# Logit columns from whole weight words, by single-precision transposes with the turned block stationary

## The chip, the cores and the metric

One NeuronCore of a Trainium2 chip runs the whole kernel. The metric is the time of one execution on the device, in microseconds. The engines are TensorE (PE, matmuls, and PEld for its weight loads), VectorE (DVE), ScalarE (ACT), GpSimd (POOL) and SyncE (SP, which issues most DMAs).

## The reference

Three layers follow each other. Tokens are 4 sequences of 768, the model width is 384 (8 heads of 48).

```
# 1: linear attention with a complex decay, per head
S = a_n[t] * S + k[t] v[t]^T          # a_n: (a_re, a_im), clipped to magnitude 0.999
y[t] = q[t] . Re(S)
# 2: gated dense layer
x = y / rms(y) * rms_g
h = silu(x @ w_gate) * (x @ w_val)    # 384 -> 1536
x2 = h @ w_out                        # 1536 -> 384
# 3: one of 8 experts per token
logits = x2 @ moe2_w_gate             # 384 -> 8
e = argmax(logits);  p = softmax(logits)[e]
out = p * (relu(x2 @ w1[e]) @ w2[e])  # 384 -> 1024 -> 384
```

The weights of layer 2 arrive as 64-bit words that the kernel turns into single precision itself.

## The kernel before, in words

Tokens go through layers 1 and 2 in 12 units of 256. `elem(u)` computes decays and phases of unit u (ACT and DVE), spreads them over heads by DMAs (tile `QK`), `attention(u)` computes scores, outputs and normalised activations `xh`, `xl` (a rounded part and the rest, so that fast matmuls keep precision), `dense(u)` runs 12 features f of 128 hidden columns: stage 1 (L850) makes gate and value columns, stage 2 (L873) adds the product with the output weights into two PSUM accumulators. `finish(u)` stores the result and its expert's place. Then the eight experts run (L1299, L1317).

`convert` makes one block of 384x384 weights: DMA of the words into `st`; a memset of a `raw` buffer (L418); `top`, a widening copy of the high part (L395 on ACT, L397 on POOL); `join`, a shift and an or on DVE (L401), after which `raw` holds the whole single-precision word; `high`, the rounded copy into `w` (L406, L408); then the rest, either `low` on DVE or POOL (L411) or, for the blocks w00 and wo0, on PE (L430, L431) with ACT copies (L434). There are twelve blocks: w00 to w03 (gate), w10 to w13 (value), wo0 to wo3 (output). Only two `raw` buffers exist (NRAW=2), and other temporary tiles live in them too. The words of a block are fetched only when the block five places back has had its `top` (AHEAD=5).

From unit 1 on, stage 2 also makes the 8 expert logits: the output weights have 8 more columns, `w_out @ moe2_w_gate`. `logit_columns` makes them per output block: it turns the 9 sub-blocks (L450, each half of the split weight against the identity), copies them out (L454), multiplies with the gate matrix stationary (L460), copies (L465), turns the result back (L466), and writes its rounded part (L471) and the rest (L473). Unit 0 computes its logits from its output instead (L893, L897).

`keep_warm` (L1388) is 15 batches of 8 matmuls whose results nobody reads. Each needs a converted third of w00, w10, w01, w11 or w02; each has the last due time of all; all write one of the two PSUM buffers that the dense accumulators take later.

The order of all this is made by a planner, `Plan.issue`, in Python at build time. A step names engines with estimated costs, what it reads and writes, and a due time. At each turn the planner takes the engine on which some step could start earliest, and of the steps that could start there at that time the one with the lowest due time. A step gets its buffers when it is issued, if enough are free. A step's DMA goes into SP's queue in the planned order. Due times come from the constants in TUNE: for example a gate block's is T0 + 3 FT g + CG + C0g, and the logit columns' before was that of unit 1 plus LC + C3g. There are three PSUM banks of the kind `t` (`bank()`), two accumulators `a`, three buffers `m`.

Of the kernel before, what the change touches and what calls it, by code (L numbers as in the profile page):

```python
# [30 lines left out]
TUNE = dict(T0=771.62, PER=649.53, FT=4.77, A0=-422.97, A1=-431.72, A2=-35.5, E0=-1137.13, E1=236.14, E2=1375.6,  # L31
            E3=785.18, CG=483.05, CO=263.88, LC=-203.35, NRAW=2, AHEAD=5, DH=547.2, FI=-16.42, RP=-1165.15, TOL=0,
            S2L=28.66, NS=3, NH=3, HOP=0.2, W1=107.43, ATP=2, PA0=0, PA1=0.08, PE0=0, PE1=0.24, RG=1, LB=-24.77,
            EB=-56.74, RB=6.57, HB=-60.28, MB=-8.8, TB=10.11, AX=1, EE=-12.66, EL=7.32, BEG=0.7, DL=2, FN=8,
            FF=15, LW=1, LO=1, C00=-926.96, C01=-266.61, C02=382.08, C03=-259.36, C10=-529.22, C11=-373.75, C12=-583.49,
            C13=1773.0, C20=-587.24, C21=781.76, C22=1957.05, C23=2500.91, C30=583.92, C31=-599.84, C32=-15.96, C33=-423.27,
            AU1=282.87, AU2=-63.05, AU3=-787.85, AU4=-777.43, EU0=224.54, EU1=294.16, EU2=16.71, EU3=-24.77,
            EU4=41.45, EU5=43.43, AC=73.5, AC0=4.7)
# [212 lines left out]
def kernel(ctx, tc, qT, kT, reT, imT, v, wg, wv, wo, rg, w2g, w1, w2, out):  # L251
# [129 lines left out]
    def convert(name, src, n, due, by_pe):  # L381
# [59 lines left out]
    def logit_columns(w, due, after):  # L441

        pr, rows, pl, wts = bank(P, P), Buf(k_raw, shape=[P, P]), bank(P, P), Buf(k_raw, shape=[P, KD, KD, P])
        for q in range(KD):
            pw = bank(P, KD, P)

            def turn(e, q=q, pw=pw):
                for j in range(KD):
                    for i in range(2):
                        TE.matmul(pw.t[:, j, :], lhsT=w.t[:, q, i, j * P:(j + 1) * P], rhs=identr,  # L450
                                  start=(i == 0), stop=(i == 1))

            add((TE, 0.68), turn, r=[(w, 0), IDENTR] + lows(w), w=[pw], due=due, after=after)
# [3 lines left out]
        def prod(e):  # L457
            for j in range(KD):
                for q in range(KD):
                    TE.matmul(pr.t[LG * q:LG * (q + 1), :], lhsT=w2gt[:, j, :], rhs=wts.t[:, q, j, :],  # L460
                              start=(j == 0), stop=(j == KD - 1))

        n = LG * KD
        s = add((TE, 1.1), prod, r=[(wts, q) for q in range(KD)] + [W2G], w=[pr], due=due)
        add((A, act(P)), lambda e: e.activation(rows.t[:n], pr.t[:n], AF.Copy), r=[pr], w=[rows], due=due)  # L465
        add((TE, mm(P, 2)), lambda e: TE.transpose(pl.t[:, :n], rows.t[:n], ident[:n, :n]), r=[rows], w=[pl], due=due)  # L466

        def cols():
            return pl.t[:, :n].rearrange("p (q l) -> p q l", l=LG)[:, :, :E]

        add((A, act(3 * E)), lambda e: e.activation(w.t[:, :, 0, DM:], cols(), AF.Copy),  # L471
            r=[pl], w=[(w, 2)], due=due)
        add((V, dve(3 * E)), lambda e: e.tensor_tensor(  # L473
            out=w.t[:, :, 1, DM:], in0=cols(), in1=w.t[:, :, 0, DM:], op=ALU.subtract),
            r=[pl, (w, 2)], w=[(w, 3)], due=due)
        return [s]
# [853 lines left out]
    with tc.manual_schedule():  # L1330
# [39 lines left out]

        q = {0: elem(0)}
# [5 lines left out]
        for g in range(FF // WB):  # L1377
            for n, w in enumerate((wg, wv)):
# [3 lines left out]
                              g < TUNE["LO"]))  # L1382
# [174 lines left out]
```

## Time and profile before

| | us |
|---|---|
| median of 3 runs (lowest, highest) | 935.14 (935.04, 936.3) |
| profiled execution, whole | 936.97 |
| its span in the trace | 935.3 |
| PE busy | 896.5 |
| DVE, ACT, POOL busy | 613.2, 518.0, 181.6 |

All times inside the trace count from the span's start. A busy PE is not PE at its peak: matmuls overlap, and a group's own duration is longer than the distance to the next group's start. The cost of a group is therefore read as the distance from its start to the start of what follows it without a hole.

### The profile page before, as it was taken

The numbers are of one execution on the slowest core, as the hardware profiler recorded it, in microseconds if no ns is written. First come the engines' busy times: TensorE is split into PE (matmuls) and PEld (weight loads), VectorE is DVE, ScalarE is ACT, GpSimd is POOL, SyncE is SP. The second block draws the span as 40 slices with busy tenths as digits, with TensorE's granted clock in tenths as the row PEclk, the third lists the DMA queues.
The fourth block names the chain that finished last, engine by engine and source line by source line (L and its number), as shares of the span: only waits on it lengthen the run. The fifth ranks groups of instructions, "written<-read, shape, count | busy, mean of one in ns | idle before, by whom it ended". The sixth has DMA issues, their size and how long they took to land.

```text
span 935.3 us, 17743 instructions
## 1 busy us (share of the span) xinstructions
PE 896.5 (96%) x6747; PEld 863.5 (92%) x6747; DVE 613.2 (66%) x1528; ACT 518.0 (55%) x996; POOL 181.6 (19%) x226
## 2 busy tenths in 40 slices
PE   2699999999999999999999999999999999999996
PEld 2689999999999999999999999999989989999996
DVE  5699867778777768686868777546566642545510
ACT  7787876675655656655656565424426433544421
POOL 3232302010111010110201020101242532222121
PEclk9899999999999999999999999999999999999999
DMA  9955233423333140605050421102346753545200
GB/s 331 292 196 140 65 78 82 102 83 77 95 61 94 45 127 18 154 18 154 17 137 19 92 80 40 48 1 66 93 122 200 219 144 111 151 129 182 91 23 23
DMA packets 68363, 98.12 MB, mean 105 GB/s; under 512 B 16038, under 2 KB 49257, under 8 KB 68276
## 3 DMA queue, kind: packets, MB, share of 16 engines
q1 hardware_dynamic: 57316, 86.61, 32.9%
q0 software_dynamic: 10688, 9.95, 3.9%
q8 instruction: 54, 0.88, 0.4%
q10 hardware_dynamic: 272, 0.40, 0.1%
q14 instruction: 33, 0.27, 0.1%
HBM read 68.19 MB, written 10.15 MB: 84 GB/s over the span
## 4 chain that ended last, share of the span: by engine, by line
PE 68%; DVE 11%; issue 8%; DMA 5%; ACT 5%; POOL 2%; SPq 0%; POOLq 0%; DVEq 0%; ACTq 0%
PE m L850 25%; PE a L873 15%; PE a L1317 7%; PE m L1299 7%; PE t L680 4%; PE t L720 3%; DVE ee L541 2%; PE t L724 1%; DMA out_dram<-eo,idx 1%; PE t L698 1%; POOL out_dram L1325 1%; DMA QK<-qk 1%; DMA rawb<-in_w_dram 1%; DVE re L576 1%; DVE rs L785 1%
## 5 line engine op out<-in xcount | busy, mean ns | idle before, releaser
L850 PE MATMUL m<-xh,w 128*128 128x256 f32 x1728 | 276.6, 285 | 1.1 <-DVE s L862 0.6
L850 PEld LDWEIGHTS m<-xh,w 128*128 128x128 f32 x1728 | 234.6, 188 | 5.7 <-issue 3.4
L873 PE MATMUL a<-wo,hh 128*128 128x392 f32 (+1 forms) x576 | 151.8, 345 | 0.0
L850 PE MATMUL m<-xl,w 128*128 128x256 f32 x864 | 149.1, 281 | 0.0
L850 PEld LDWEIGHTS m<-xl,w 128*128 128x128 f32 x864 | 122.3, 188 | 0.0
L873 PEld LDWEIGHTS a<-wo,hh 128*128 128x128 f32 x576 | 100.5, 188 | 0.7 <-issue 0.7
L873 PE MATMUL a<-wo,hl 128*128 128x392 f32 (+1 forms) x288 | 98.3, 341 | 1.7 <-DVE hl L867 1.7
L865 ACT ACTIVATE hh<-s 128x256 fp32r<-128x256 f32 x144 | 59.5, 415 | 72.9 <-PE a L873 45.7
L857 ACT ACTIVATE s<-m 128x256 f32<-128x256 f32 x144 | 54.6, 380 | 77.8 <-PE m L850 40.1
L867 DVE TENSOR_TENSOR hl<-s,hh 128x256 fp32r<-128x256 f32 x144 | 66.6, 467 | 29.4 <-ACT hh L865 28.7
L859 DVE SCALAR_TENSOR_TENSOR s<-s,m 128x256 f32<-128x256 f32 x144 | 59.4, 413 | 21.3 <-ACT s L857 21.1
L1325 POOL DMA_INDIRECT out_dram<-eo,idx x28 | 37.2, 1330 | 157.7 <-ACT eo L1323 91.2
L1308 DVE SCALAR_TENSOR_TENSOR ehl<-m,ehh 128x384 fp32r<-128x384 f32 (+6 forms) x64 | 35.2, 555 | 44.6 <-ACT ehh L1306 44.0
L862 DVE SCALAR_TENSOR_TENSOR s<-s,m 128x256 f32<-128x256 f32 x144 | 59.6, 415 | 2.1
L1323 ACT ACTIVATE eo<-a,eg 114x384 f32<-114x384 f32 (+5 forms) x28 | 16.3, 582 | 74.9 <-PE a L1317 60.6
L873 PEld LDWEIGHTS a<-wo,hl 128*128 128x128 f32 x288 | 54.1, 188 | 2.3 <-DVE hl L867 2.3
L1306 ACT ACTIVATE ehh<-m 128x384 fp32r<-128x384 f32 (+6 forms) x64 | 31.2, 491 | 44.8 <-PE m L1299 41.7
L720 PE MATMUL t<-AK,vt 128*64 128x224 f32 (+3 forms) x384 | 49.6, 346 | 0.5 <-ACT raw L465 0.3
L680 PE MATMUL t<-QK 96*128 96x128 f32 x384 | 48.1, 276 | 0.3 <-DMA QK<-ee 0.3
L680 PEld LDWEIGHTS t<-QK 96*128 96x128 f32 x384 | 46.3, 192 | 1.3 <-issue 0.8
L948 POOL DMA_INDIRECT slots<-tid,sl x24 | 25.0, 1043 | 115.7 <-DVE cnt L943 111.8
L690 DVE TENSOR_TENSOR AK<-t,mask 128x512 f32<-128x512 f32 x40 | 26.9, 686 | 21.3 <-PE t L680 21.1
(290 smaller groups left out, 1853.0 us busy)
## 6 DMA issues: line engine op xcount, KB each, us to landing
rawb<-in_w_dram SPq DMA_DIRECT2D x21, 512.0 KB
rawb<-in_w_dram SPq DMA_DIRECT2D x28, 384.0 KB
QK<-qk SPq DMA_DIRECT2D x24, 290.2 KB
QK<-ee SPq DMA_DIRECT2D x24, 290.2 KB
re<-in_a_re_dram SPq DMA_DIRECT2D x12, 384.0 KB
im<-in_a_im_dram SPq DMA_DIRECT2D x12, 384.0 KB
qk<-in_q_dram SPq DMA_DIRECT2D x12, 384.0 KB
qk<-in_k_dram SPq DMA_DIRECT2D x12, 384.0 KB
```

The source lines that it names most:

```text
L680: TE.matmul(sc.t[:, i, :], lhsT=K(4 * g + i), rhs=Q(4 * g + i), start=True, stop=True)
L720: TE.matmul(yt.t[64 * n:64 * n + d, i, :n_], lhsT=vs[:, o:o + d], rhs=ak.t[:, 2 * i + n, :n_], start=True, stop=first)
L850: TE.matmul(ps.t[:, i, :], lhsT=W1[i, g].t[:, k, part, fs], rhs=x.t[:, k, :], start=(n == 0), stop=(n == 3 * KD - 1))
L857: add((A, act(U)), lambda e: e.activation(s.t, ps.t[:, 0, :], AF.Tanh, scale=0.5), r=[ps], w=[s], due=dh, table=AF.Tanh)
L859: add((V, dve(U)), lambda e: e.scalar_tensor_tensor(out=s.t, in0=s.t, scalar=1.0, in1=ps.t[:, 0, :], op0=ALU.add, op1=ALU.mult), r=[s, ps] ...
L862: add((V, dve(U)), lambda e: e.scalar_tensor_tensor(out=s.t, in0=s.t, scalar=0.5, in1=ps.t[:, 1, :], op0=ALU.mult, op1=ALU.mult), r=[s, ps ...
L865: add((A, act(U)), lambda e: e.activation(hh.t, s.t, AF.Copy), r=[s], w=[hh], due=dh)
L867: lambda e: e.tensor_tensor(out=hl.t, in0=s.t, in1=hh.t, op=ALU.subtract), r=[s, hh], w=[hl], due=dh, lock=True)
L873: TE.matmul(acc[t].t[:, :wide], lhsT=h.t[:, ts_], rhs=WO[g].t[:, k3, part, :wide], start=(f == 0 and n == 0), stop=(f == KF - 1 and n == 2))
L1299: TE.matmul(ps.t, lhsT=w.t[:, k, fs], rhs=y.t[:, k, :], start=(i == 0), stop=(i == 3 * KD - 1))
L1317: TE.matmul(po.t, lhsT=h.t[:, f, js], rhs=w.t[:, f, :], start=(f == 0 and i == 0), stop=(f == KF2 - 1 and i == 2))
L1325: add((G, 1.05), lambda e, o=o, j=j: e.indirect_dma_start(out=outs[(x + j) % len(outs)], out_offset=bass.IndirectOffsetOnAxis(ap=at(j), ax ...
```

## The change

The logit columns are made inside `convert`, from `raw` right after `join`, with a fixed due time of -900. The turn is a transpose of the whole single-precision word. In the product the turned 128x128 block is stationary and the 8 columns of the gate matrix move, so that the result comes out in the layout in which it is stored. The memset of an output block's `raw` waits for the previous output block's columns (`columns[-1:]`). The planner's cost of `top` changes from the costs in `light` to 1.5 us on ACT or POOL. Constants of the first units' due times are set anew.

```diff
-TUNE = dict(... A0=-422.97, A1=-431.72, E0=-1137.13, E1=236.14, E2=1375.6, CG=483.05, CO=263.88,
-  C00=-926.96, C01=-266.61, C02=382.08, C03=-259.36, C10=-529.22, C11=-373.75, C12=-583.49, C13=1773.0,
-  C20=-587.24, C21=781.76, C22=1957.05, C23=2500.91, AU1=282.87, AU2=-63.05, AU3=-787.85, AU4=-777.43,
-  EU0=224.54, EU1=294.16, EU2=16.71, AC0=4.7)
+TUNE = dict(... A0=-236.46, A1=-472.46, E0=-1089.45, E1=15.79, E2=877.26, CG=103.16, CO=113.49,
+  C00=-777.21, C01=-334.11, C02=848.02, C03=-298.01, C10=-263.13, C11=145.29, C12=-365.28, C13=1663.04,
+  C20=-609.73, C21=617.47, C22=2200.34, C23=2893.59, AU1=-150.32, AU2=-90.58, AU3=-723.11, AU4=-2.5,
+  EU0=203.4, EU1=237.13, EU2=616.42, AC0=467.29)
...
-    def convert(name, src, n, due, by_pe):
+    def convert(name, src, n, due, by_pe, rows=None, after=()):
...
-        add((G, 0.08 + N * 0.96e-3), lambda e: e.memset(raw.t, 0.0), w=[raw], due=due - 2, lock=True)
-        paces.append(add(light, top, r=pairs, w=[raw], due=due, lock=True))
+        add((G, 0.08 + N * 0.96e-3), lambda e: e.memset(raw.t, 0.0), w=[raw], due=due - 2, lock=True, after=after)
+        paces.append(add([(A, 1.5), (G, 1.5), (V, dve(N), TUNE["RB"])], top, r=pairs, w=[raw], due=due, lock=True))
         add((V, dve(N)), join, r=pairs + [raw], w=[raw], due=due, lock=True)
         add(light, high, r=[raw], w=[(w, 0)], due=due, lock=True)
+        if rows is not None:
+            rows.append(logit_columns(w, raw, -900))
...
-    def logit_columns(w, due, after):
-        pr, rows, pl, wts = bank(P, P), Buf(k_raw, shape=[P, P]), bank(P, P), Buf(k_raw, shape=[P, KD, KD, P])
+    def logit_columns(w, raw, due):
+        wts, pl = Buf(k_raw, shape=[P, KD, KD, P]), bank(P, KD, E)
         for q in range(KD):
             pw = bank(P, KD, P)
             def turn(e, q=q, pw=pw):
                 for j in range(KD):
-                    for i in range(2):
-                        TE.matmul(pw.t[:, j, :], lhsT=w.t[:, q, i, j * P:(j + 1) * P], rhs=identr,
-                                  start=(i == 0), stop=(i == 1))
-            add((TE, 0.68), turn, r=[(w, 0), IDENTR] + lows(w), w=[pw], due=due, after=after)
+                    TE.transpose(pw.t[:, j, :], raw.t[:, q, j * P:(j + 1) * P], ident)
+            add((TE, 0.4), turn, r=[raw], w=[pw], due=due)
...
         def prod(e):
-            for j in range(KD):
-                for q in range(KD):
-                    TE.matmul(pr.t[LG * q:LG * (q + 1), :], lhsT=w2gt[:, j, :], rhs=wts.t[:, q, j, :],
+            for q in range(KD):
+                for j in range(KD):
+                    TE.matmul(pl.t[:, q, :], lhsT=wts.t[:, q, j, :], rhs=w2gt[:, j, :E],
                               start=(j == 0), stop=(j == KD - 1))
...
-        s = add((TE, 1.1), prod, r=[(wts, q) for q in range(KD)] + [W2G], w=[pr], due=due)
-        add((A, act(P)), lambda e: e.activation(rows.t[:n], pr.t[:n], AF.Copy), r=[pr], w=[rows], due=due)
-        add((TE, mm(P, 2)), lambda e: TE.transpose(pl.t[:, :n], rows.t[:n], ident[:n, :n]), r=[rows], w=[pl], due=due)
+        add((TE, 1.1), prod, r=[(wts, q) for q in range(KD)] + [W2G], w=[pl], due=due)
...
-        s = []
-        for g in range(FF // WB):
-            s = logit_columns(WO[g], due_moe(1, 3 * g) + TUNE["LC"] + TUNE[f"C3{g}"], s)
```

## Rows read from the trace of the kernel before

**Rows 1.** The page, busy us of PE and PEld, share of span, instructions

```profile
PE 896.5 (96%) x6747; PEld 863.5 (92%) x6747; DVE 613.2 (66%) x1528; ACT 518.0 (55%) x996; POOL 181.6 (19%) x226
```

**Rows 2.** Busy by stretch: length, engines' busy us, PEclk, DMA share, GB/s

```profile
0.00:60.00 60.00, 34.94 (x231) 28.79 (x232) 39.63 (x60) 46.37 (x66) 21.05 (x50) 0.94 0.95 313
...
60.00:300.00 240.00, 238.56 (x2001) 230.51 (x2000) 188.12 (x481) 163.34 (x314) 41.16 (x55) 1.00 0.35 87
...
30.00:40.00 10.00, 4.79 (x26) 4.65 (x25) 6.77 (x6) 7.49 (x9) 1.18 (x2) 0.67 1.07 222
```

**Rows 3.** Timeline of PE, start: start us, us, operation, [idle before <- releaser]

```profile
29.58 2.12 PE L450 MATMUL t<-identr,wo 128*128 128x128 f32 x18
36.91 4.59 PE L1388 MATMUL a<-w,identr 128*128 128x384 f32 x16 [5.21 <-ACT w L406]
...
42.01 1.80 PE L680 MATMUL t<-QK 96*128 96x128 f32 x14 [0.28 <-DMA QK<-ee]
...
66.44 0.52 PE L850 MATMUL m<-xh,w 128*128 128x256 f32 x3
```

**Rows 4.** Timeline of PE, 73 to 84 us

```profile
73.02 3.07 PE L1388 MATMUL a<-w,identr 128*128 128x384 f32 x16
75.93 0.52 PE L850 MATMUL m<-xh,w 128*128 128x256 f32 x3
...
82.32 1.57 PE L1388 MATMUL a<-w,identr 128*128 128x384 f32 x8
83.73 0.51 PE L873 MATMUL a<-wo,hh 128*128 128x384 f32 x2
```

**Rows 5.** Timeline of PE, 91 to 140 us, turns and products with their followers

```profile
91.12 2.12 PE L450 MATMUL t<-identr,wo 128*128 128x128 f32 x18
93.08 0.57 PE L850 MATMUL m<-xh,w 128*128 128x256 f32 x3
...
102.37 0.86 PE L460 MATMUL t<-raw,w2gt 128*32 128x128 f32 x18
103.15 0.59 PE L720 MATMUL t<-AK,vt 128*64 128x224 f32 x4
...
121.57 1.55 PE L450 MATMUL t<-identr,wo 128*128 128x128 f32 x12 [0.50 <-DVE rs L782]
...
132.22 0.82 PE L893 MATMUL t<-ident,x 128*128 128x128 f32 x6
132.79 0.87 PE L450 MATMUL t<-identr,wo 128*128 128x128 f32 x6
...
138.80 0.73 PE L897 MATMUL t<-w2gt,raw 128*128 128x8 f32 x6
139.39 0.60 PE L850 MATMUL m<-xh,w 128*128 128x256 f32 x3
```

**Rows 6.** Instructions on the gate matrix: ns min/median/max, first and last start us

```profile
L460 PEld LDWEIGHTS t<-raw,w2gt x72: 106/110/110, 51.7 to 136.3; 128*32 128x32 f32 x72
...
L897 PEld LDWEIGHTS t<-w2gt,raw x12: 188/192/192, 138.7 to 142.0; 128*128 128x128 f32 x12
```

**Rows 7.** Timeline of all engines, raw buffers between 20 and 61 us

```profile
20.94 1.15 POOL L418 MEMSET raw<- 128x1152 f32 x1 [0.27 <-PE t L430]
...
25.02 1.34 DVE L401 SCALAR_TENSOR_TENSOR raw<-wo,raw 128x1152 int32<-128x1152 int32 x1
...
29.70 1.06 POOL L418 MEMSET raw<- 128x1152 f32 x1 [2.09 <-PE t L430]
...
32.88 1.50 ACT L395 ACTIVATE raw<-w 128x1152 f16<-128x1152 bf16 x1 [0.59 <-DMA w<-in_wv_dram]
...
36.89 2.63 DVE L411 TENSOR_TENSOR w<-raw,w 128x1152 fp32r<-128x1152 f32 x2 [1.12 <-ACT w L406]
38.34 1.26 ACT L454 ACTIVATE raw<-t 128x384 f32<-128x384 f32 x3 [0.43 <-DVE w L411]
...
60.73 1.07 POOL L418 MEMSET raw<- 128x1152 f32 x1 [0.87 <-PE t L466]
```

More of the change, by code (lines that the diff above doesn't have):

```diff
@@ L29 @@
 TABLE_LOAD = 1.3
-TUNE = dict(T0=771.62, PER=649.53, FT=4.77, A0=-422.97, A1=-431.72, A2=-35.5, E0=-1137.13, E1=236.14, E2=1375.6,
-            E3=785.18, CG=483.05, CO=263.88, LC=-203.35, NRAW=2, AHEAD=5, DH=547.2, FI=-16.42, RP=-1165.15, TOL=0,
+TUNE = dict(T0=771.62, PER=649.53, FT=4.77, A0=-236.46, A1=-472.46, A2=-35.5, E0=-1089.45, E1=15.79, E2=877.26,
+            E3=785.18, CG=103.16, CO=113.49, LC=-203.35, NRAW=2, AHEAD=5, DH=547.2, FI=-16.42, RP=-1165.15, TOL=0,
             S2L=28.66, NS=3, NH=3, HOP=0.2, W1=107.43, ATP=2, PA0=0, PA1=0.08, PE0=0, PE1=0.24, RG=1, LB=-24.77,
             EB=-56.74, RB=6.57, HB=-60.28, MB=-8.8, TB=10.11, AX=1, EE=-12.66, EL=7.32, BEG=0.7, DL=2, FN=8,
[L35 to L38, printed above, removed]
+            FF=15, LW=1, LO=1, C00=-777.21, C01=-334.11, C02=848.02, C03=-298.01, C10=-263.13, C11=145.29, C12=-365.28,
+            C13=1663.04, C20=-609.73, C21=617.47, C22=2200.34, C23=2893.59, C30=583.92, C31=-599.84, C32=-15.96, C33=-423.27,
+            AU1=-150.32, AU2=-90.58, AU3=-723.11, AU4=-2.5, EU0=203.4, EU1=237.13, EU2=616.42, EU3=-24.77,
+            EU4=41.45, EU5=43.43, AC=73.5, AC0=467.29)
 HOP = TUNE["HOP"]
@@ L457, in prod @@
         def prod(e):
-            for j in range(KD):
-                for q in range(KD):
-                    TE.matmul(pr.t[LG * q:LG * (q + 1), :], lhsT=w2gt[:, j, :], rhs=wts.t[:, q, j, :],
+            for q in range(KD):
+                for j in range(KD):
+                    TE.matmul(pl.t[:, q, :], lhsT=wts.t[:, q, j, :], rhs=w2gt[:, j, :E],
                               start=(j == 0), stop=(j == KD - 1))
-        n = LG * KD
-        s = add((TE, 1.1), prod, r=[(wts, q) for q in range(KD)] + [W2G], w=[pr], due=due)
-        add((A, act(P)), lambda e: e.activation(rows.t[:n], pr.t[:n], AF.Copy), r=[pr], w=[rows], due=due)
-        add((TE, mm(P, 2)), lambda e: TE.transpose(pl.t[:, :n], rows.t[:n], ident[:n, :n]), r=[rows], w=[pl], due=due)
[L468 to L474, printed above, removed]
+        add((TE, 1.1), prod, r=[(wts, q) for q in range(KD)] + [W2G], w=[pl], due=due)
+        add((A, act(KD * E)), lambda e: e.activation(w.t[:, :, 0, DM:], pl.t, AF.Copy), r=[pl], w=[(w, 2)], due=due)
+        return add((V, dve(KD * E)), lambda e: e.tensor_tensor(
+            out=w.t[:, :, 1, DM:], in0=pl.t, in1=w.t[:, :, 0, DM:], op=ALU.subtract),
             r=[pl, (w, 2)], w=[(w, 3)], due=due)
-        return [s]
     k_re, k_im, k_ta, k_tb = (Slots(right, n, [P, KD, U], F32) for n in ("re", "im", "ta", "tb"))
@@ L1369 @@
         add((A, act(P)), lambda e: e.activation(NEGR.t, ident, AF.Copy, scale=-1.0), w=[NEGR], due=40)
+        columns = []
         q = {0: elem(0)}
@@ L1381 @@
             WO.append(convert(f"wo{g}", words(wo)[g * WB:(g + 1) * WB], XW, due_moe(0, 3 * g) + TUNE["CO"] + TUNE[f"C2{g}"],
-                              g < TUNE["LO"]))
+                              g < TUNE["LO"], columns, columns[-1:]))
         fill = Buf(k_a, shape=[P, WB])
```

## The prediction, made before the changed kernel was built

> **What bounds the kernel now.** I read the page's busy shares first: TensorE (PE) is busy 896.5 of 935.3 us, 96% [rows 1]. Then busy time by stretch: of the first 60 us PE is busy 34.94, of the next 240 it is busy 238.56 [rows 2]. So there are two regimes. Up to about 66 us the kernel runs on latency: loads, the element-wise chain of the first unit, its attention. PE idles or runs the warm-keeping matmuls of L1388. From the first stage-1 matmul at 66.44 us [rows 3] PE is a queue without holes, and the end moves by exactly the PE time added to it or taken from it, or by a later start of it. The reader should see in PE's timeline that even behind 66 us not everything is useful: three batches of warm-keeping matmuls stand from 73.02 to 75.93 and from 82.32 to 83.73, together 2.91 + 1.41 = 4.32 us [rows 4]. They cannot be dropped: the accumulators of stage 2 take the PSUM place that these matmuls write, and the first L873 begins exactly where the last batch ends.
>
> The sum is made against the profiled execution (936.97 us, span 935.3). The median of the runs shown is 935.14, 1.83 lower, so I subtract 1.83 at the end.
>
> **The change part by part, per block of 384 output-weight rows.**
>
> *Turn.* Removed: 18 matmuls of the two word halves against the identity (L450). Undisturbed they take from 91.12 to 93.08, 1.96 us [rows 5]. Added: 9 single-precision transposes of 128x128. The same instruction stands at L893: six of them from 132.22 to 132.79, 0.57 us, 0.095 each [rows 5]. Nine make 0.86. Gain 1.10 us.
>
> *Product.* Removed: 9 products with the 32-column gate matrix stationary (18 records, L460), 102.37 to 103.15, 0.78 us. Added: 9 products with the turned 128x128 block stationary and 8 moving columns. The same shape is L897: three products, six records, 138.80 to 139.39, 0.59 us, so 0.197 each and 1.77 for nine [rows 5]. Loss 0.99 us.
>
> The row of the weight loads shows why: a load for L897 lasts 188 to 192 ns, one for L460 106 to 110 [rows 6]. The Trainium skill, TensorE: Matmul & The Clock Gate, section LDWEIGHTS (loading the stationary operand), says that a load costs its number of columns over 1.2 GHz; by that an estimate of the product is 18 x 0.107 = 1.92 us per block instead of 1.77, and the block's net gain would shrink by 0.15. Direction and ratio agree with the rows. The spacing of the records (0.098) is the better price, and I use it.
>
> *Second turn.* The 96x96 transpose back and its copy go. On PE that is about 0.1 us; its record is hidden among neighbours, so I bound it at 0 to 0.2.
>
> Net per block: 1.10 - 0.99 + 0.1 = about 0.2, between 0.1 and 0.4. Before, blocks 1 to 3 stand in the full queue (91, 120 and 128 to 133 us) while block 0 stands at 29.6 us and later in holes [rows 3, 5]. After, blocks 1 to 3 still follow their words' conversion, whose due times (1517, 3114, 3822 worked out from the constants, against 1832, 3021, 3579) still lie behind most of the other conversions. So I count three blocks in the queue: 0.6 us saved. One hole of 0.50 us inside a split turn (121.57, waiting for VectorE) [rows 5] goes too, because the new turn waits for the words alone and has a quarter of the steps to fit in. Together 1.1 us, bounds 0.3 to 1.8. If one block slipped ahead of 66 us, another 2.63 would be hidden; I don't count it.
>
> *ACT and DVE.* Three evacuations of 128x384 stay (1.26 us for three [rows 7]); one 96x128 copy goes. Their due time of -900 puts them ahead of everything, the first unit's element-wise steps included. In the queue stretch they cost nothing as long as PE has stage-1 work, at most 3 x 1.26 = 3.8 us of ACT time if it has none.
>
> *Raw places.* Two buffers hold words in conversion, and the logit columns take them too. Before, block 0's turned words took one place at 38.34 and its second buffer gave the place back only at 60.73, when the memset of the next conversion stopped waiting for L466 [rows 7]. For 22 us the twelve conversions ran through one place. After, the second buffer is gone and the turned words leave as soon as the product has run. This is the possible gain beyond PE time: the third to last warm-keeping batches wait for converted words (ACT w L406 [rows 3]), so words that come earlier move batches out of the queue into holes ahead of 66 us. Bounds: 0 to 4.32 us, and below zero if conversions come later. I take one batch, 1.4 us.
>
> *Order of the conversions.* By the constants, the new order is w00, wo0, w12, w01, w10, w03, w11, wo1, w02, w13, wo2, wo3 (before: w00, wo0, w12, w10, w11, w01, w03, w02, wo1, wo2, w13, wo3). The words of w02, which the last warm-keeping batches need, fall from eighth to ninth place. That is why I take one batch and not three. On the SP queue the same seven weight blocks go out before the first unit's spread; their order among themselves changes, the bytes don't. Loads for the second unit's elements (due 1024, before 1302) pass w11 (1034), a block of three DMAs; nothing there ends last before 66 us.
>
> *The added wait.* The memset of each output block's words now waits for the previous block's columns. Behind it on POOL stand only gathers and masks, which the planner issues in between. It strings wo1, wo2, wo3 in a row, about 10 us each (conversion and columns). They need not be ready before stage 2 of their features; with the chain starting near 70 us the last would be ready near 105, where it is today. Price zero, 1 to 3 us if each slips by a further 5 us.
>
> *Costs told to the planner* (1.5 us for the widening copy) are closer to the rows: L395 lasts 1.50 [rows 7]. This moves some copies from ACT to POOL. I count zero, from -1 to +1.
>
> **Sum.** 1.1 + 1.4 = 2.5 us less: 936.97 - 2.5 = 934.5 in the profile's terms, 932.6 in the median's.
>
> **Rivals.**
>
> *Rival 1, nothing that can be measured.* The PE saving (1.1) comes, the batches stay where they are, and the reordered start is late or early by under a microsecond. For: the sum's certain part is only 1.1 us. Against: all due times of the start move at once, and an exact tie would be chance. Time 934.0, within 0.2% (1.87 us), which is what a measurement of this kernel can tell from no change.
>
> *Rival 2, slower: the transposes lock the banks.* Place: the first output block, at 26 to 40 us. Its words are joined at 25.02; the turn may start right then, and its three outputs take all three PSUM banks of their kind. The copies that empty them need a raw place. One holds wo0 itself; the other was taken at 20.94 by the memset of the next conversion, which gets its words only at 32.88 and ends with L411 at 36.89 + 2.63 = 39.5 [rows 7]. Until then the banks are full, so the remainders of wo0 (L430) can't run, and wo0 keeps its own place, which before came free at 29.70 [rows 7]. PE then idles from about 28 to 39 and falls to the low clock: in 30 to 40 us the mean granted clock is already 0.67, with 5.2 us idle [rows 2, 3]. When the copies run at last, the product, due -900, goes ahead of the first scores: 1.77 us at 2.4 GHz, up to 3.5 at 1.2. Scores that began at 42.01 [rows 3] would begin near 44, and the queue with them: +2.2 us. The second and third weight conversions start 10 to 15 us later than before, which may push one more batch into the queue, +1.4. Less 1.1: +2.5, so 937.6. It decides when the delay of the scores is over 1.1 us. For it: the release times in the rows, and that the planner gives out a bank without looking whether its copy has a place. Against: w12 may be through earlier when the copies go to POOL, the hold of 22 us behind 38 us is gone, and the attention chain (24 us from 42 to 66) may absorb part.
>
> *Rival 3, a large gain.* If conversions run ahead far enough that all three batches leave the queue and one output block is turned before 66 us: 1.1 + 4.3 + 2.6 = 8.0, so 927.1. For it: the 22 us with one place. Against: w02 is ninth, and VectorE and ACT are as busy as before.
>
> **Chances and range.** Forecast 0.42 (its own range 930.5 to 933.2), rival 1 0.25, rival 2 0.27, rival 3 0.06. Faster by over 0.2%: forecast and rival 3, 0.48; within: 0.25; slower: 0.27. For eight in ten the range reaches from 928.5, two thirds of the way to rival 3, to 939.0, rival 2 with 1.4 us more for a second batch.
>
> **What would show it.** L450 and L466 are gone, nine transposes take 0.86 us and 18 records of the product 1.77. Right: the first L850 at 66 us or sooner, under 3 us of L1388 behind it. Rival 2: a hole of 8 us or more in PE between 27 and 40 us, scores after 43. Wrong in the large: holes in PE behind 70 us, which would mean that the strung conversions of wo1 to wo3 are late; or a first L850 moved by more than 3 us either way, which no row here prices.

## The result, and the profile after

The changed kernel takes 948.36 us (median of 4 runs, 947.51 to 949.07), the kernel before 935.72 beside it: ratio 1.0131, 95% interval 1.0113 to 1.015. It is slower by 12 us where 2.5 us less were forecast. Line numbers of the code behind `logit_columns` are lower by 8 or 9: L850, L873, L680, L720, L805, L1088, L1299, L1388 are now L841, L864, L671, L711, L796, L1079, L1290, L1380; the new turn is L451, the new product L460.

The span grew from 935.3 to 946.9 us. Three marks in TensorE's timeline split the 11.6 us: the first stage-1 product, the last stage-2 group (683.65 before, 692.63 after), the end.

| stretch | before | after | more |
|---|---|---|---|
| start to first stage-1 product | 66.44 | 74.94 | 8.5 |
| to the last stage-2 group | 617.2 | 617.7 | 0.5 |
| to the end | 251.6 | 254.3 | 2.6 |

Page of the kernel after, busy us (share) x instructions; it answers to [rows 1]:

```profile
PE 902.6 (95%) x6707; PEld 867.4 (92%) x6707; DVE 615.6 (65%) x1530; ACT 510.7 (54%) x988; POOL 183.8 (19%) x228
```

Busy time by stretch, kernel after (columns as in [rows 2]):

```profile
0.00:60.00 60.00, 33.71 (x172) 27.82 (x173) 32.72 (x49) 43.20 (x59) 21.20 (x50) 0.89 0.89 293
60.00:300.00 240.00, 235.79 (x1928) 226.55 (x1928) 189.08 (x473) 152.81 (x303) 39.65 (x54) 1.00 0.35 92
30.00:40.00 10.00, 3.38 (x18) 2.78 (x16) 6.69 (x7) 5.35 (x6) 2.85 (x3) 0.92 1.07 229
41.00:52.00 11.00, 10.63 (x49) 9.19 (x49) 4.51 (x5) 6.45 (x8) 3.72 (x7) 0.50 0.97 349
```

There are fewer TensorE records (6707 against 6747), yet 6 us more busy time: from 41 to 52 us the clock stands at its lower level, 0.50 (1.2 of 2.4 GHz), while before it was 1.00 from 42 on. The first unit's scores, key transposes and output products account for most of it: the same instructions take 5.0 us more of TensorE's time than before. Timeline of TensorE, kernel after, against [rows 3]:

```profile
41.08 2.53 PE L671 MATMUL t<-QK 96*128 96x128 f32 x8 [7.70 <-DMA QK<-qk]
...
44.04 3.67 PE L671 MATMUL t<-QK 96*128 96x128 f32 x16
...
67.03 4.45 PE L1380 MATMUL a<-w,identr 128*128 128x384 f32 x24
71.32 0.49 PE L796 MATMUL t<-ident,y 128*128 128x128 f32 x3
73.95 1.23 PE L451 MATMUL t<-ident,raw 128*128 128x128 f32 x9 [2.14 <-DVE raw L401]
74.94 0.60 PE L841 MATMUL m<-xh,w 128*128 128x256 f32 x3
```

The first scores begin no later than before (41.08 against 41.34). But the hole ahead of them is 7.7 us (before 5.2), and no keep-warm batch stands between it and them, as 16 products did before. L796 turns a chunk's normalised result: chunk 0's went from 57.84 to 61.62 (3.8 later), chunk 1's from 63.31 to 71.32 (a further 4.2), and the step from there to stage 1 grew by 0.5. So the 8.5 us arise in attention of the first unit.

The new instructions themselves came out near their forecast. TensorE, kernel after, turn and product with their followers, against [rows 5]:

```profile
95.28 2.07 PE L460 MATMUL t<-w2gt,raw 128*128 128x8 f32 x18
97.20 0.60 PE L841 MATMUL m<-xh,w 128*128 128x256 f32 x3
...
132.39 1.16 PE L451 MATMUL t<-ident,raw 128*128 128x128 f32 x9
133.30 0.60 PE L841 MATMUL m<-xh,w 128*128 128x256 f32 x3
```

A turn is 0.91 us (0.86 forecast), a product 1.92 (1.77).

Of the 2.6 us at the end, 2.0 are idle time of TensorE at 713 to 723 us. Kernel after: issue of expert 1's words on SP's queue; the chain of waits behind it; busy time by stretch:

```profile
703.47 2.44 SPq L1079 DMA_DIRECT2D rawb<-in_w_dram  x3
```
```profile
704.76 12.11 DMA rawb<-in_w_dram
```
```profile
712.98:722.98 10.00, 7.98 (x64) 7.34 (x64) 7.81 (x14) 7.61 (x16) 1.54 (x1) 1.00 0.63 180
```

Before, this load went out at 685.07, and in the ten microseconds that answer to these TensorE was busy throughout:

```profile
704.00:714.00 10.00, 10.00 (x79) 10.00 (x78) 8.40 (x16) 7.59 (x16) 2.02 (x1) 1.00 0.68 202
```

### The profile page after: what moved, and what is told of

It reads as the page before. It is cut to its first block, busy times and chain, and to the rows that moved or that the text cites. A ratio compares the mean times of both kernels' runs of the same rounds, so it can differ in the third digit from the quotient of the medians.

```text
span 946.9 us, 17658 instructions
## 1 busy us (share of the span) xinstructions
PE 902.6 (95%) x6707; PEld 867.4 (92%) x6707; DVE 615.6 (65%) x1530; ACT 510.7 (54%) x988; POOL 183.8 (19%) x228
## 4 chain that ended last, share of the span: by engine, by line
PE 69%; DVE 10%; issue 8%; DMA 5%; ACT 5%; POOL 1%; SPq 0%; POOLq 0%; DVEq 0%; ACTq 0%
PE m L841 25%; PE a L864 15%; PE a L1308 7%; PE m L1290 6%; PE t L671 5%; PE t L711 4%; DMA rawb<-in_w_dram 2%; PE t L715 2%; DVE ee L532 1%; PE a L1380 1%; PE t L689 1%; POOL out_dram L1316 1%; DMA QK<-qk 1%; DMA out_dram<-eo,idx 1%; DVE re L567 1%
## 5 line engine op out<-in xcount | busy, mean ns | idle before, releaser
L841 PE MATMUL m<-xh,w 128*128 128x256 f32 x1728 | 277.5, 285 | 1.5 <-DVE s L853 1.2
L841 PEld LDWEIGHTS m<-xh,w 128*128 128x128 f32 x1728 | 234.5, 188 | 6.6 <-issue 3.6
L864 PE MATMUL a<-wo,hh 128*128 128x392 f32 (+1 forms) x576 | 151.8, 345 | 0.0
L841 PE MATMUL m<-xl,w 128*128 128x256 f32 x864 | 149.1, 281 | 0.0
L841 PEld LDWEIGHTS m<-xl,w 128*128 128x128 f32 x864 | 122.3, 188 | 0.0
L864 PEld LDWEIGHTS a<-wo,hh 128*128 128x128 f32 x576 | 100.4, 188 | 0.6 <-issue 0.5
L864 PE MATMUL a<-wo,hl 128*128 128x392 f32 (+1 forms) x288 | 98.3, 341 | 1.4 <-DVE hl L858 1.4
L850 DVE SCALAR_TENSOR_TENSOR s<-s,m 128x256 f32<-128x256 f32 x144 | 59.2, 413 | 20.2 <-ACT s L848 20.0
L1299 DVE SCALAR_TENSOR_TENSOR ehl<-m,ehh 128x384 fp32r<-128x384 f32 (+6 forms) x64 | 35.1, 556 | 43.8 <-ACT ehh L1297 43.8
L671 PE MATMUL t<-QK 96*128 96x128 f32 x384 | 52.1, 289 | 7.8 <-DMA QK<-qk 7.7
L671 PEld LDWEIGHTS t<-QK 96*128 96x128 f32 x384 | 49.6, 203 | 10.1 <-issue 8.6
L864 PEld LDWEIGHTS a<-wo,hl 128*128 128x128 f32 x288 | 54.1, 188 | 1.8 <-DVE hl L858 1.8
L711 PE MATMUL t<-AK,vt 128*48 128x224 f32 (+3 forms) x384 | 50.5, 351 | 0.3
```

The costliest lines, as they stand in the source:

```text
L671: TE.matmul(sc.t[:, i, :], lhsT=K(4 * g + i), rhs=Q(4 * g + i), start=True, stop=True)
L711: TE.matmul(yt.t[64 * n:64 * n + d, i, :n_], lhsT=vs[:, o:o + d], rhs=ak.t[:, 2 * i + n, :n_], start=True, stop=first)
L841: TE.matmul(ps.t[:, i, :], lhsT=W1[i, g].t[:, k, part, fs], rhs=x.t[:, k, :], start=(n == 0), stop=(n == 3 * KD - 1))
L850: add((V, dve(U)), lambda e: e.scalar_tensor_tensor(out=s.t, in0=s.t, scalar=1.0, in1=ps.t[:, 0, :], op0=ALU.add, op1=ALU.mult), r=[s, ps] ...
L864: TE.matmul(acc[t].t[:, :wide], lhsT=h.t[:, ts_], rhs=WO[g].t[:, k3, part, :wide], start=(f == 0 and n == 0), stop=(f == KF - 1 and n == 2))
```

## The experiments

Theories. **C**: the new columns cost time (they hold raw places, the product is longer). **D**: the new due times do. **K**: the hole and the low clock do. **B**: the keep-warm batches among attention's steps do. **L**: the place of the weight blocks in memory does, for the end. **O**, formed on the way: the instructions are neutral, and what costs is any change in the order that the planner writes out, which fits the code of before and no other.

| kernel | ratio to before, interval | stage 1 starts | first to last | to the end |
|---|---|---|---|---|
| after | 1.0131 [1.0113, 1.015] | 74.94 | 617.7 | 254.3 |
| e1 | 1.0122 [1.0104, 1.0141] | 72.94 | 621.3 | 249.7 |
| e2 | 1.0149 [1.013, 1.0169] | 71.56 | 626.5 | 252.4 |
| e3 | 1.0202 [1.0178, 1.0225] | 72.40 | 627.4 | 251.9 |
| e5 | 1.007 [1.0049, 1.0091] | 73.62 | 617.5 | 251.8 |
| f1 | 1.0108 [1.0063, 1.0152] | 74.49 | 618.3 | 251.8 |
| f2 | 1.0086 [1.0056, 1.0116] | 73.85 | 618.5 | 252.8 |
| f3 | 1.011 [1.0069, 1.0151] | 71.23 | 621.5 | 252.0 |
| f4 | 1.0025 [1.0008, 1.0042] | 68.56 | 617.0 | 249.9 |
| p1 | 1.009 [1.0059, 1.0122] | 74.62 | 620.3 | 249.2 |
| p2 | 1.0067 [1.004, 1.0094] | 67.59 | 620.9 | 252.2 |
| p3 | 1.0084 [1.0061, 1.0108] | 67.10 | 625.2 | 249.9 |
| p4 | 1.0271 [1.0243, 1.0299] | 81.39 | 628.9 | 250.7 |
| g1 | 1.0091 [1.0067, 1.0115] | 66.33 | 627.2 | 252.0 |
| g2 | 1.0086 [1.0057, 1.0115] | 68.50 | 617.2 | 250.5 |
| g3 | 1.0129 [1.0109, 1.015] | 74.51 | 618.0 | 252.8 |
| e4 | 1.021 [1.019, 1.0231] | 69.41 | 632.3 | 252.4 |
| x1 | 0.997 [0.9955, 0.9985] | 67.24 | 615.5 | 250.0 |
| x2 | 1.0075 [1.0049, 1.0102] | 68.64 | 621.0 | 251.8 |

The last three columns are of one profiled run each. The first scores wait for DMAs: in the kernel after they begin at 41.08, in three kernels that differ from it by nothing ahead of them (e5, f2, g3) at 39.35, 40.75 and 39.42. So a difference of under 2 us between two starts says little.

**e1 and e2: code and due times apart.** e1 is the new code with the TUNE of before, e2 the old code with the new TUNE.

```diff
e1  -TUNE = dict(... CG=103.16, CO=113.49 ... AC0=467.29)   +TUNE = dict(... CG=483.05, CO=263.88 ... AC0=4.7)
e2  -TUNE = dict(... CG=483.05, CO=263.88 ... AC0=4.7)      +TUNE = dict(... CG=103.16, CO=113.49 ... AC0=467.29)
```

e1: 

> The changed code with all the early due times of the kernel before. Theory D (the due times make the dense stage start late): the first stage-1 product comes back to 66 to 69 us from 74.94 and the time to 934 to 938. Theory C (the code itself: both raw places are held by the first output block's columns until 28 to 33 us, so the words of the next blocks are converted some 8 us later and queries and scores find TensorE cold): the first stage-1 product stays at 73 to 77 and only the 2.6 us at 704 to 717 go, 944 to 948. In both the weights of expert 1 are asked for near 694 or before, because the block w10 is placed ahead of w01 again.

e2: 

> The code of the kernel before with all the new due times. Theory D: the dense stage starts at 73 us or later, 944 to 950. Theory C: it starts at 65 to 69 us, and what is left is the late load of expert 1's weights (w01 placed ahead of w10), 935 to 940.

Either half alone costs as much as the whole. e1 came out as C had it (72.94, 947.51) and e2 near what D had (71.56, 950.46), while each theory was to leave the other kernel near before. Neither is enough alone.

**e5: place.** The tile of w10 is taken ahead of w01's.

```diff
+        if s.name == "w01":
+            s.where[0].tile(s.shape, s.dtype, name="w100", tag="w100", bufs=1)
```

> The changed kernel, with the place of w10 taken ahead of that of w01, and nothing else. Theory L (the expert's word block for expert 1 lies on w10's place, which the last join uses until 703 us): its load goes out at 685 to 695 instead of 703.47, the wait at 704 to 717 is gone, 945.3 to 946.3 (2.0 to 3.0 us less). If the load has another reason: 948 as before, load at 703.

Kernel e5, SP's queue, and busy time in the ten microseconds that answer to 712.98 above:

```profile
692.51 1.49 SPq L1081 DMA_DIRECT2D rawb<-in_w_dram  x3
```
```profile
711.43:721.43 10.00, 10.00 (x79) 10.00 (x79) 8.59 (x16) 7.59 (x16) 2.02 (x1) 1.00 0.67 200
```

L holds for the load and the hole: every instruction stands in the order of the kernel after, the load goes out 11 us earlier, the hole is gone, and the end lasts 251.8 us as before. How much that is worth is less sure. In all eight kernels whose load goes out at 703 us or later the end lasts 251.8 to 254.3, in the twelve others 249.2 to 252.2; the middle values are 1.8 us apart, and 2.5 is the figure of one pair. The medians differ by 5 us (943.32 against 948.36), more than the 2 to 3 that were expected. Of the 4.0 by which the profiled runs differ, 2.5 lie in the end and 1.3 in the start, whose first scores began 1.7 earlier (39.35).

**e3, f1, f2, f3, f4: clock and batches.** e3 lets all batches read w00, which the planner then orders anew. f1 and f3 emit 36 keep-warm products right ahead of the first scores; f2 and f3 leave out the nine batches of 51.9 to 71.3 us; f4 leaves out, in the kernel before, the 16 products of 36.91 us. f1 to f4 keep the rest of the order as it is.

```diff
e3  -order = [(W1[i, g], k) for g in range(4) for i in range(2) for k in range(KD)]
e3  +order = [(W1[0, 0], k) for _ in range(8) for k in range(KD)]
f1  +for k in range(36 if u == c == g == 0 else 0):
f1  +    TE.matmul(state["fill"].t, lhsT=identr, rhs=W1[0, 0].t[:, k % KD, 0, :WB], start=True, stop=True)
f2  +if 4 <= state["kw"] <= 12:      # f4: 4 to 5
f2  +    return
```

e3: 

> The changed kernel, but all keep-warm batches read the weight block w00, which is ready from about 24 us, in place of the eight blocks in turn; the products of a batch stay the same. Theory K (the hole of TensorE at 33.4 to 41.1 us and the low clock behind it are what attention pays for): batches fill the hole, the granted clock of 40 to 50 us rises from 0.50 to 0.9 or more, the scores at 44.04 take 2 us instead of 3.67, the first stage-1 product comes 3 to 8 us earlier, 940 to 945. If the hole is only a symptom (attention waits for its own steps of the other engines): clock up, start within 1.5 us of 74.94, 946 to 949.

f1: 

> The changed kernel in its own order on every engine; only 36 more keep-warm products (reading w00, result unused) stand on TensorE right ahead of the first scores of attention 0, in the hole of 33.4 to 41.1 us. Theory K (the hole lets the clock fall, and scores, key transposes and state products between 41 and 52 us then take twice their time, some 5 us): granted clock near 1.00 from 40 to 50 instead of 0.50, the 16 scores in 2.0 us or less instead of 3.67, first stage-1 product at 69 to 72, time 943 to 946. Theory B (the batches that stand in TensorE's queue between attention's steps from 52 to 72 us set its pace): clock up, but first stage-1 product within 1.5 us of 74.9, 947 to 950.

f2: 

> The changed kernel in its own order, but the nine keep-warm batches of 51.9 to 71.3 us are left out (13 us of them stand in the chain of waits there). Theory B: attention's two chunks end earlier, first stage-1 product at 67 to 71, time 941 to 946 as far as the clock holds. Theory K: the batches only fill time in which attention waits for ScalarE, VectorE and GpSimd; the start moves by less than 2 us and the clock of 55 to 75 falls, 948 to 953.

f3: 

> Both edits together: 36 products in the hole, no batches from 51.9 to 71.3 us. If theories K and B both hold and add up, the first stage-1 product is back at 65 to 68 and the time at 938 to 942. If the order of the steps itself (not clock, not batches) is what makes attention late, the start stays at 71 or later and the time at 944 or more.

f4: 

> The kernel before in its own order, without the two keep-warm batches (16 products) at 36.91 us that stand ahead of its first scores. Theory K: the clock stays at 0.50 through the scores and behind them, the first stage-1 product moves from 66.4 to 69 to 72, time 938 to 942. Theory B: the start stays within 1 us, 935 to 937.

Kernel f4, TensorE, and busy time with clock:

```profile
41.60 4.09 PE L680 MATMUL t<-QK 96*128 96x128 f32 x16 [11.10 <-DMA QK<-qk]
...
68.56 0.52 PE L850 MATMUL m<-xh,w 128*128 128x256 f32 x3
```
```profile
41.60:46.00 4.40, 4.40 (x20) 4.13 (x21) 1.36 (x1) 3.00 (x4) 1.95 (x4) 0.50 0.97 267
46.00:47.00 1.00, 1.00 (x11) 1.00 (x10) 0.70 (x2) 1.00 (x2) 0.61 (x1) 0.97 0.83 306
```

This prices K by itself, for a low clock that ends at 46 us: it costs some 2 us at the start of stage 1 (68.56 against 66.44), and the time rises by 0.25% (2.3 us). In the kernel after the low clock lasts to 52 us. With the order kept, a late start is passed on whole: the last stage-2 group is 1.9 us later too.

In f1 the fill ended 1.6 us ahead of the scores and the clock was 0.64 from 45 to 50 us all the same, so f1 decides little. f2 splits the two: the start moved by 1.1 us and the clock from 55 to 75 us fell to 0.54 and less, as K had it, but its time, 945.56, lies in B's range. f3 shows more. Kernel f3, TensorE:

```profile
56.94 0.90 PE L798 MATMUL t<-ident,y 128*128 128x128 f32 x3 [0.18 <-ACT y L793]
...
66.39 0.90 PE L798 MATMUL t<-ident,y 128*128 128x128 f32 x3 [4.58 <-ACT y L793]
69.43 2.15 PE L451 MATMUL t<-ident,raw 128*128 128x128 f32 x9 [2.13 <-DVE raw L401]
71.23 0.99 PE L843 MATMUL m<-xh,w 128*128 128x256 f32 x3
```

Chunk 0 is 4.7 us earlier than in the kernel after, even ahead of before (57.84). So clock and batches together explain the lateness of chunk 0. Chunk 1 still trails it by 9.45 us (5.47 before), and TensorE, now idle between, meets stage 1 at the low clock. The time hardly moved. e3 says less, since its order is new: the clock was 1.00 from 40 to 60 us, but six batches stood among attention's steps from 45 to 58 us, the clock was 0.74 from 60 to 72 us, and it takes 6 us more than the kernel after.

**p1 to p4: one part of the change alone, on the kernel before.**

```diff
p1  -paces.append(add(light, top, ...))    +paces.append(add([(A, 1.5), (G, 1.5), (V, dve(N), TUNE["RB"])], top, ...))
p2  -AC0=4.7                               +AC0=467.29
p3  -s = logit_columns(WO[g], ...)         +convert(f"wo{g}", ..., None if g == 0 else columns, columns[-1:])
p4  -s = logit_columns(WO[g], ...)         +convert(f"wo{g}", ..., columns if g == 0 else None, columns[-1:])
```

p1: 

> The kernel before, with one part of the change alone: the planner's entries for the first step of a word conversion (1.5 us on ScalarE and on GpSimd, the full VectorE time in place of half). No instruction is added or removed, only the order written out for the queues moves. Theory O (the order of the first 75 us is what the time hangs on, and any edit that moves it costs): the first stage-1 product moves from 66.4 to 69 or later, 938 to 944. If only the new columns and due times matter: 935 to 937.

p2: 

> The kernel before, with one due time alone set anew: that of the second chunk of attention 0 (AC0 467.29 in place of 4.7). Theory D1 (this puts conversions ahead of the second chunk's copies, and is the 4.2 us by which chunk 1 trails in the changed kernel): the transposes of chunk 1's result come 8 us or more behind those of chunk 0 instead of 5.5, first stage-1 product at 69 to 71, 938 to 942. If chunk 1 trails for another reason: within 1 us of before, 935 to 937.

p3: 

> The kernel before with the new columns for output blocks 1 to 3 alone: block 0 keeps the old columns, due times and the planner's entries for the conversions are those of before, so that the queues of the first 65 us are as before. This prices the new turn and product in the dense stage. Theory S (the sizes of the prediction hold but for the product at 1.9 us): start at 66.4, time within 3 us of before, 933 to 939. Theory C (the new columns cost in the dense stage because they hold the raw places): the span between the first stage-1 product and the last stage-2 group of unit 11 grows from 613.3 by 3 us or more, 939 to 944.

p4: 

> The kernel before with the new columns for output block 0 alone; blocks 1 to 3 keep the old columns, due times and planner's entries are those of before. Theory C0 (block 0's columns made early from its raw words hold both raw places until 28 to 33 us, and all that follows in the first 75 us is ordered behind that): first stage-1 product at 72 or later, 941 to 948. If block 0's place is harmless: start within 1.5 us of 66.4, 934 to 938.

All four are slower, and three by more than any range written for them (p1 946.25, p2 943.59, p4 962.12). p1 adds no work and is slower by 0.9%: stage 1 starts at 74.62, as late as in the kernel after. But more than the order moves, other than its expectation says: with the new entries the planner gives five of the twelve widening copies to GpSimd, one before (the kernel after has five too). The price is that of order and choice of engine together. Nor is it late by the same steps: its first scores begin at 43.48 and the clock is 0.50 from 48 to 56 us, so chunk 0 is 8.0 us late and chunk 1 a further 2.3, where the kernel after has 3.8 and 4.2. p2 has chunk 1 8.3 us behind chunk 0 and loses mainly behind the start. p3 has the start of before and loses 8 us in the dense stage (617.2 us before; the 613.3 of the expectation are near the busy part of it). Busy time in the stretch from 100 us behind the first stage-1 product on, before, then kernel p3:

```profile
166.44:216.44 50.00, 50.00 (x410) 48.48 (x408) 38.94 (x112) 32.19 (x68) 7.33 (x11) 1.00 0.32 81
```
```profile
167.10:217.10 50.00, 48.00 (x370) 45.67 (x368) 35.74 (x100) 29.72 (x60) 4.39 (x8) 1.00 0.32 80
```

From the first stage-1 product to the last stage-2 group TensorE idles for 8.4 us in p3 and 4.4 before. That is half of the loss. A lower clock (0.83 from 127 to 137 us) is worth an estimated 1.7 us (10 us at 0.83); the rest is not told apart. p3 does not say which of its three parts did it, the early due time, the wait for the previous block's columns or the raw places: none was tried alone.

p4 shows C's mechanism at its worst, and it is the lock that the prediction's second rival described. Kernel p4, TensorE, then ScalarE, then POOL:

```profile
24.68 1.17 PE L488 MATMUL t<-ident,raw 128*128 128x128 f32 x9 [1.79 <-DVE raw L401]
...
39.52 0.77 PE L708 MATMUL t<-QK 96*128 96x128 f32 x2 [10.87 <-DMA QK<-ee]
...
42.27 3.85 PE L497 MATMUL t<-w2gt,raw 128*128 128x8 f32 x18
...
62.35 0.82 PE L432 MATMUL t<-raw,ident 128*128 128x384 f32 x2
```
```profile
37.42 1.26 ACT L491 ACTIVATE raw<-t 128x384 f32<-128x384 f32 x3 [1.49 <-DVE w L411]
```
```profile
46.18 1.06 POOL L418 MEMSET raw<- 128x1152 f32 x1 [2.36 <-PE t L497]
```

The memset of the next conversion takes the second raw place at 20.76. The turns of block 0 (L488) fill the three banks at 24.68, and their copies (L491) run only at 37.42, when that conversion ends with its L411. The product stands among the scores and takes 3.85 us at the low clock. It holds its raw place until 46.2, so the fourth conversion begins there instead of at 29.70 ([rows 7]). The remainders of wo0 (L432) begin at 62.35 instead of 26.51. In the kernel after, the copies stand at 24.00 and the product at 25.95, ahead of the next memset, and the raw places come free at 28.17 and 33.27; in e1, with the due times of before, the product stands at 25.34. What brings it forward are probably the planner's new entries for the conversions: with them wo0's words are joined at 20.65 (after), 20.05 (e1) and 20.39 (p1), with the old ones at 25.02 (before) and 23.19 (p4). No run isolates this, since e1 differs from p4 in blocks 1 to 3 too.

**g1, g2, g3, e4: can the loss be had back?** g1 is the new code with due times chosen once more, g2 the same for old columns on wo0 and new ones on the rest. In both the planner is told 1.92 us for the product. g3 puts one state product of chunk 1 on VectorE, e4 one due time back.

```diff
g1, g2  -add((TE, 1.1), prod, ...)    +add((TE, 1.92), prod, ...)
g1      +TUNE = dict(... E2=1514.01, RP=-535.07, W1=90, FF=12, C00=-1259.96, C02=552.79, AU2=-8.7 ... AC0=5.68)
g2      +TUNE = dict(... CG=132.7, W1=125, FF=12, C10=-219.47, C11=-264.63, C12=-142.63 ... AC0=19.15)
g3      -lambda e: e.tensor_tensor(out=S2.t, ...)    +lambda e: (V if u == 0 else e).tensor_tensor(out=S2.t, ...)
e4      -AC0=467.29                                  +AC0=4.7
```

g1: 

> The changed code for all four blocks, the product entered in the planner with the 1.92 us that it takes, and early due times chosen once more for this code (the order of the first 100 us is another one). Theory O (the loss is order: it can be had back): first stage-1 product at 66 to 70 us, span of the dense stage 614 to 619 as before, 935 to 941. Theory C (the columns hold raw places and their product is 1 us longer, whatever the order): 943 or more.

g2: 

> Old columns for block 0, new ones for blocks 1 to 3, the product entered with 1.92 us, early due times chosen for this mixture, w10 and w11 placed ahead of w01. Theory O: the 7 us that the same code lost on the old due times go, start at 65 to 68, 933 to 938, no more than 2 us from before either way, since a block's new turn and product save and add about the same (turn 1.96 to 0.9, product 0.78 to 1.92). Theory C: 940 or more.

g3: 

> The changed kernel; only the state product that chunk 1 of attention 0 waits for goes to VectorE instead of GpSimd, at its place in the order. Theory G (GpSimd's 1.87 us against 0.55 us on VectorE delay chunk 1): the products that read it at 60.7 come 1.2 us or more earlier and the dense stage starts 0.5 to 2 us earlier, 946 to 948. If other work (batches, conversions on ScalarE ahead of the copy of YT) ends last: start within 0.5 us of 74.94, 948.

e4: 

> The changed kernel with one due time put back: that of the second chunk of attention 0 (AC0 4.7 in place of 467.29). Theory D1 (it is what makes chunk 1 trail by 9.7 us): the transposes of chunk 1's result come 6 to 7.5 us behind chunk 0's, first stage-1 product at 71 to 73; the time falls to 944 to 947 if nothing in the dense stage depends on that order, and stays if the conversions that gave way are late there instead.

g3 has no effect, but it does not answer the question. On VectorE the state product takes 0.55 us instead of 1.87, but it stands behind the steps of chunk 0's norm and ends at 59.88, 3.5 us behind the copy that it reads; on GpSimd it ended 2.0 us behind it (59.37). In f2 and f3, where no batches stand ahead, TensorE does wait for it, 1.39 and 2.03 us. g1 and e4 were the surprise. The medians of g1 (945.7) and g2 (943.49) lie in the ranges written for C. g1 starts stage 1 at 66.33, as before, and still ends 0.9% late. Kernel g1, TensorE:

```profile
66.33 0.90 PE L841 MATMUL m<-xh,w 128*128 128x256 f32 x3 [0.46 <-ACT xh L802]
...
78.10 1.01 PE L841 MATMUL m<-xh,w 128*128 128x256 f32 x3 [2.51 <-DVE s L853]
...
129.61 0.44 PE L864 MATMUL a<-wo,hl 128*128 128x384 f32 x1 [1.43 <-DVE hl L858]
```

In its place the dense stage has 13.3 us of idle time (4.4 before), most of it in waits of 0.6 to 2.5 us for VectorE, for a chunk's copies, for the scores' DMA. e4 starts 5.5 us earlier than the kernel after and ends 7 us later. The first stage-1 product is a mark at which lateness can be read, not its cause: work that is pushed past it comes back as holes. g2's six runs lie between 937.86 and 948.54; the profiled one, at 936.2 us span, with 617.2 us from first to last and three of the new blocks in it, shows that this mixture can come near before, but not that it does.

**x1 and x2: new instructions in the old order.** Both keep the order of the kernel before, instruction by instruction.

```diff
x1, x2  -for i in range(2):
x1, x2  -    TE.matmul(pw.t[:, j, :], lhsT=w.t[:, q, i, j * P:(j + 1) * P], rhs=identr, start=(i == 0), stop=(i == 1))
x1, x2  +TE.transpose(pw.t[:, j, :], w.t.bitcast(F32)[:, q, 0, j * P:(j + 1) * P], ident)
x2      +TE.matmul(pr.t[:, P + E * q:P + E * (q + 1)], lhsT=wts.t[:, q, j, :], rhs=w2gt[:, j, :E], ...)
```

x1: 

> The kernel before in its own order; at each turn of an output block nine single-precision transposes of the high part stand in place of the 18 products (the low part is left out of the turned block). Theory O (the sizes of the prediction hold where the order stays: a turn 1.96 to 0.9 us, three of them in the full queue): 2.7 to 3.4 us less than before, 932 to 934, first stage-1 product within 0.7 us of 66.4. Theory C (the new instructions themselves are what costs): no gain or a loss, 936 or more.

x2: 

> As the one before it, and at each product of an output block the 18 matrix products of the new form (turned block stationary, 8 columns) stand ahead of the old ones, which stay, so that the new product is paid for on top. Theory O: three new products of 1.9 us in the full queue against three turns that save 1.1 each, and a fourth product among attention's steps that costs 0 to 2: 2 to 5 us more than before, 938 to 941, of which the old products are 3 x 0.8. Theory C: 943 or more.

Kernel x1, then x2, TensorE:

```profile
91.94 1.15 PE L449 MATMUL t<-ident,wo 128*128 128x128 f32 x9
92.84 0.60 PE L848 MATMUL m<-xh,w 128*128 128x256 f32 x3
```
```profile
130.08 2.07 PE L458 MATMUL t<-w2gt,raw 128*128 128x8 f32 x18
132.08 0.85 PE L462 MATMUL t<-raw,w2gt 128*32 128x128 f32 x18
132.87 0.33 PE L449 MATMUL t<-ident,wo 128*128 128x128 f32 x1
```

The turn takes 0.90 us, 1.06 less than before; three of them are 3.2 us, and x1 is faster by 0.3% (2.8 us; median 933.46 against 936.12). x2 is 9.8 us above x1 (1.05% of 936), and its median of 944.0 lies in the range that was written for C, not in O's. What O's range had too small can be read: four new products of 2.0 to 2.24 us make 8.3, and the one among attention's steps, at 51.59, is followed by a low clock that stretches its neighbours by 1.4 (the old product 1.43 us instead of 0.78, the three groups behind it 1.81 instead of 1.03). O had that fourth product at 0 to 2 us. These 9.7 us match the medians; the two profiled runs differ by 8.7, of which 1.4 lie in the start, 5.5 in the dense stage and 1.8 in the end, where no product stands. In the full queue a block's new turn and product so cost 2.90 (0.90 + 2.00) where the old ones cost 2.75 (1.96 + 0.79) and a second turn: zero, within 0.2 us. C fails as a price of instructions in the full queue. O's first half, neutral instructions, holds there; its second half is borne out by the ten other kernels with an order of their own (e1 to e4, p1 to p4, g1, g2), all slower by 0.67% or more, though none of them separates the order from the choice of engines.

## Why the prediction was wrong

**The instructions: right.** The turn was forecast at 0.86 and measured at 0.91, the product at 1.77 and 1.92, a block's net saving at 0.2 and now about zero. In the product the record's spacing misled: 0.098 us, taken from three products in a row, against 0.107 over eighteen. The Trainium skill, TensorE: Matmul & The Clock Gate, section LDWEIGHTS (loading the stationary operand), lets a load take its columns over 1.2 GHz, by which the prediction gave an estimate of 1.92; the trace agrees with the page, and the prediction's choice of the shorter price was wrong by 0.15 a block. "Direction and ratio agree with the rows" was right in the direction alone: the records of the two loads stand as 1.8 to 1 (188 to 192 against 106 to 110 ns), the columns as 4 to 1.

**The step that failed: the reordered start was priced near zero.** It was "late or early by under a microsecond" in rival 1 and one batch better in the forecast. The first stage-1 product came 8.5 us later: 3.8 at chunk 0 of the first attention, 4.2 more at chunk 1, 0.5 behind it. "Costs told to the planner ... I count zero, from -1 to +1": alone they cost 8.4 us (p1). A first L850 moved by more than 3 us was named as what "no row here prices", and left out of range and chances. Yet the change moved 27 constants of due times, the planner's entries for twelve conversions and the place of four column steps. The runs show that such a move has a price of its own, here 6 to 25 us for one part (p1, p2, p3, p4), and that it is not the sum of its parts: the four parts add to 48 us, the whole costs 12.

**The strung conversions: zero was right here.** The last block's memset came 12.6 us later (111.46 against 98.83), and the dense stage grew by 0.5 us all the same. The 8 us of p3 are those of another set of due times.

**The batch of 1.4 us: wrong.** Three batches stood in the queue before ([rows 4]); three still do, 4.25 us from 87.83 to the first L864 at 92.08.

**Rival 2: right in its mechanism, which did not happen here.** The lock of the banks is real: p4 shows it step by step, with a hole of 10.9 us and a time 2.7% longer. In the changed kernel no bank was locked, because the copies of block 0 got the second raw place ahead of the next conversion: its turns ran at 22.16 and 23.79, its product at 25.95. Of the signs, the hole (7.7 us) and the low clock came, the late scores did not (41.08). So its time, 937.6, had the right sign by another way. f4 prices 4.4 us of attention at the low clock at 2.1 to 2.3; the changed kernel has 11 us of it, which no run prices alone. What the rival lacked is that no batch was left ahead of the scores, behind which the clock had risen before, that chunk 1 fell a further 4.2 us behind, and the end.

**The end: not seen at all.** Which tile a block's place is taken for first decides which of them an expert's words later lie on, and so when their load may go out. That w01 came ahead of w10 cost 2.5 us at 713 us in the profiled pair, 640 us behind the change (e5).

**Open.** What makes chunk 1 trail is not shown. In the kernel after the clock is 1.00 from 52.1 us on. Without the batches chunk 1 still trails by 9.41 (f2) and 9.45 us (f3), though there at 0.50 for part of the way. Its state product is not ruled out (g3). AC0 moves it (p2: 5.5 to 8.3 us, e4: 9.7 to 7.3) but does not account for all, and putting it back loses more elsewhere. The trace shows where it arises: chunk 1's output products (L711, before L720) begin at 60.28 instead of 52.45, 7.8 us later, when chunk 0 is only 3.8 late. These 4.2 us are half of the late start. Nor is it settled whether some order for the new code reaches that of before; g1 and g2 were two tries. No complete kernel here beats the kernel before. x1 does, without the low part; turning whole words at the old time would need the raw block to be kept that long, which wasn't tried.

## What to carry to other kernels

Where a planner writes the order, a change has two prices: that of its instructions, which the rows give, and that of the new order and the new choice of engines, which they don't. Put the second into the range as soon as due times, planner costs or buffers move, above all in a start that waits for many engines. To measure the first alone, emit the new instructions inside the old order (x1, x2); to price the second, change the planner's entries and no work (p1), and count which engine each step got. And read the stretch behind a mark before believing that an earlier mark is time won.

## What the runs showed of the hardware

Behind a hole the clock rose at different speed, with TensorE busy nearly throughout. Before, behind 16 keep-warm products from 36.91, it rose from 0.50 (38 to 40 us) to 1.00 at 40.3; in the kernel after it stayed at 0.50 from 41 to 52 us under scores, key transposes and the products behind them (10.63 of 11 us busy, above). Kernel x2 shows it fall without a hole, behind the 18 records of 8 columns at 51.59; busy time with clock:

```profile
52.00:53.00 1.00, 1.00 (x11) 1.00 (x11) 1.00 (x3) 1.00 (x4) 0.00 (x0) 1.00 1.03 409
53.00:54.00 1.00, 1.00 (x10) 0.98 (x13) 0.95 (x3) 0.79 (x2) 0.13 (x1) 0.74 0.95 375
54.00:55.00 1.00, 1.00 (x18) 0.79 (x15) 0.98 (x1) 0.00 (x0) 1.00 (x1) 0.50 0.23 88
```

The same product in the full queue (95.28 in the kernel after, between dense products) left it at 1.00.
